# LSH-masked attention in front of two feed-forward blocks: the hash projection of a head in four matmuls, its sum and comparison on other engines, and a new order of the attention

## The chip, the cores and the metric

The kernel runs on one core of a Trainium2 chip. The metric is the device time of one execution in microseconds (us). Five engines work side by side, each through its own queue in order: TensorE (PE) does matmuls and transposes, VectorE (DVE), ScalarE (ACT) and GpSimd (POOL) do elementwise work, SyncE (SP) issues nearly all DMAs.

## The reference

Attention over 2 x 8 heads with 768 rows of 64, where a query sees only the keys that fall in its hash bucket (six signs of a random projection), then two feed-forward blocks of 512 to 2048 to 512 over 1536 tokens:

```python
q_bits = (np.einsum('bhsd,dk->bhsk', q, proj) > 0).astype(np.int64)
k_bits = (np.einsum('bhsd,dk->bhsk', k, proj) > 0).astype(np.int64)
powers = 2 ** np.arange(n_bits)
q_bucket = np.sum(q_bits * powers, axis=-1)
k_bucket = np.sum(k_bits * powers, axis=-1)
mask = q_bucket[:, :, :, None] == k_bucket[:, :, None, :]
scores = scale * np.matmul(q, k.transpose(0, 1, 3, 2))
scores = np.where(mask, scores, -1000000000.0)
attn = softmax(scores); out = np.matmul(attn, v)
h = x @ w_in;  y = (h * np.tanh(softplus(h))) @ w_out      # first block (mish)
h = y @ w_in2; z = (elu(h)) @ w_out2                       # second block
```

## The kernel before, in words

All matmul operands are held as a rounded high part and a low part, the rest (types F32R), and a product is made of hi x hi, hi x lo and lo x hi.

*Attention.* The 16 heads are worked through in tiles of 128 query rows, 6 per head, 96 in all. `prepare(g)` readies head g: q and k come in together (rw), are split into z (high and low), and four DMAs spread z into the operand qkt. `project` (L433) multiplies z by the table sp in six matmuls of 384 columns into one PSUM bank pj: three products times two halves of the rows. One DVE instruction (`bits`, L447) compares the bank with 0 and turns the result into two rows of marks per bit, and four small DMAs (mk) carry these into qkt. They make the masked pairs of the score matmul so negative that the later maximum cuts them to one constant. Head 0 goes another way, without those DMAs.

Per tile: `scores`, four matmuls (st, L511); on DVE the maximum (L514) and its negative (nb, L517); on ACT the exponential (L519). Per pair of tiles: three groups of four transposes (tu, L570); of each group ACT casts the high part (pth, L575) and DVE subtracts the low part (ptl, helper line L260), and four value matmuls (xt, L583) use them. xt is copied out by ACT (xr), moved by DMA, summed and divided by POOL, and split into x_hi and x_lo. tu and st have two PSUM buffers each; xt and pj share two.

*Feed-forward.* Weights arrive as packed doubles (wraw) and are unpacked by `convert`, per unit in five instructions on DVE and two each on ACT and POOL (L299 to L325). Units 0, 1 and 2 are converted while the attention still runs. Then `moe` runs the two blocks (h, L696), 2220 matmuls of 512 columns.

*Order.* Every instruction is an `Op` of a planner (`Plan.run`) that knows a cost per engine, its inputs and its buffers. At each step it takes, for each engine, the ready op of the lowest priority number, and emits the program in that order. The priority of an attention op is the tile's number plus `OFF[name]` plus `ODD[name][tile % 6]` (function `order`, and `at` inside `prepare`). These tables thus set the order on every engine.

At the start, POOL clears 384 columns of x_lo (L657), ten warm-up matmuls (warm, L665) read them, and then the first head follows.

Of the kernel before, what the change touches and what calls it, by code (L numbers as in the profile page):

```python
# [9 lines left out]
F32 = mybir.dt.float32  # L10
# [191 lines left out]
def kernel(ctx, tc, qk, v, w, tab, out):  # L202
# [13 lines left out]
    NB = 6  # L216
# [136 lines left out]
    def attention(p, ap, dp, pss, pst, psx, h_r):  # L353
        ident = ap.tile([128, 128], F32, name="ident")
        cst = ap.tile([128, 3 + NR], F32, name="cst")
        sp = ap.tile([128, 2, 192], F32R, name="sp")
        least, value, small = cst[:, 0:1], cst[:, 1:2], cst[:, 2 + NR:3 + NR]
# [19 lines left out]
        bits_r = ring(2, [128, HS], F32R, "bits")  # L377
# [24 lines left out]
        def prepare(g):  # L402
# [33 lines left out]
            o = pj_op = p.op({PE: 1050}, project, [lo, first[0]], [z, pj], at('pj'))  # L436
# [212 lines left out]
        def setup():  # L649
            nc.vector.memset(f32(sp), 0.0)  # L650
# [415 lines left out]
```

## Time and profile before

| what | us |
|---|---|
| median of 3 timed runs | 744.91 (744.44 to 745.0) |
| the profiled execution, its own time | 746.06 |
| its span from first to last instruction | 744.3 |
| PE busy in the span | 733.9 |
| DVE, ACT, POOL busy | 596.4, 446.7, 389.9 |

The profile is of one execution. Busy time counts an instruction from its start to its end; neighbouring matmuls overlap, so their cost is read from start to start. The attention takes about the first 239 us, the feed-forward blocks the rest. The granted TensorE clock is full in all slices of the profile.

### The profile page before, as it was taken

The page shows a single profiled execution, that of the slowest core. Times are in us where ns is not written, and L with a number is a line of the kernel's source. Part 1 is how long each engine was busy: PE and PEld are TensorE (multiplying, and loading weights), DVE is VectorE, ACT ScalarE, POOL GpSimd, SP SyncE. Part 2 cuts the span into 40 slices and gives each one's busy share as a digit, 9 for nine tenths or more (in the row PEclk, how much of TensorE's full clock was granted, in tenths as well). Part 3 has the DMA queues.
Part 4 walks back from the last instruction along what each step waited for, and adds up shares of the span by engine and source line. Part 5 has one row for each costly group of instructions (what it writes and reads, how often), then busy time and mean ns, then how long its engine had stood idle before and what let it go on. Part 6 is the DMA issues. An engine that isn't in the chain of part 4 may idle for free.

```text
span 744.3 us, 11114 instructions
## 1 busy us (share of the span) xinstructions
PE 733.9 (99%) x3900; PEld 638.3 (86%) x3900; DVE 596.4 (80%) x1103; ACT 446.7 (60%) x871; POOL 389.9 (52%) x323
## 2 busy tenths in 40 slices
PE   8998999999999999999999999999999999999998
PEld 7998999999998878888888888888888888888887
DVE  7899999899997987487677868987665977979872
ACT  5787888888886665543353336568555554635530
POOL 4336726635657664636346274988425355263620
PEclk9999999999999999999999999999999999999999
DMA  7785866767620122122111212311201111113113
GB/s 199 195 208 151 209 148 171 189 162 193 174 63 1 58 86 85 37 83 79 57 57 56 86 59 83 107 64 58 85 28 58 57 57 57 56 62 108 58 59 112
DMA packets 26984, 72.90 MB, mean 98 GB/s; under 512 B 6048, under 2 KB 7216, under 8 KB 26928
## 3 DMA queue, kind: packets, MB, share of 16 engines
q1 hardware_dynamic: 26784, 72.17, 33.7%
q8 instruction: 31, 0.51, 0.3%
q14 instruction: 25, 0.20, 0.1%
q10 hardware_dynamic: 144, 0.01, 0.0%
HBM read 45.76 MB, written 3.19 MB: 66 GB/s over the span
## 4 chain that ended last, share of the span: by engine, by line
PE 88%; DVE 7%; ACT 3%; issue 1%; DMA 0%; POOL 0%; SPq 0%; DVEq 0%; ACTq 0%; POOLq 0%
PE h L696 47%; PE h_b L696 15%; PE xt L583 8%; PE st L511 7%; PE tu L570 7%; PE pj L433 2%; DVE ptl L260 2%; DVE pt L514 1%; ACT pt L519 1%; DVE g L260 1%; DVE T L260 1%; PE warm L665 0%; DMA rr<-dr 0%; ACT pth L575 0%; DVE x_lo L260 0%
## 5 line engine op out<-in xcount | busy, mean ns | idle before, releaser
L696 PE MATMUL h<-g,w 128*128 128x512 f32 x1140 | 264.9, 389 | 1.3 <-DVE g L260 1.3
L696 PEld LDWEIGHTS h<-g,w 128*128 128x128 f32 x1140 | 213.7, 188 | 46.4 <-DVE g L260 2.1
L696 PE MATMUL h<-x_hi,w 128*128 128x512 f32 x384 | 124.0, 390 | 0.0
L260 DVE TENSOR_TENSOR ptl<-tu,pth 128x512 fp32r<-128x512 f32 x144 | 96.1, 686 | 13.0 <-ACT pth L575 11.9
L260 POOL TENSOR_TENSOR wt<-wt,w 128x512 f32<-128x512 f32 x40 | 51.9, 1298 | 92.6 <-DVE c L309 52.7
L575 ACT CAST pth<-tu 128x512 fp32r<-128x512 f32 x144 | 79.9, 587 | 28.3 <-PE tu L570 27.7
L519 ACT ACTIVATE pt<-pt,nb 128x768 f32<-128x768 f32 x96 | 90.5, 944 | 8.3 <-DVE nb L517 7.9
L317 POOL TENSOR_TENSOR wt<-wt,ws 128x512 f32<-128x512 f32 x24 | 31.0, 1295 | 116.1 <-DVE ws L312 116.1
L514 DVE TENSOR_SCALAR_CACHE_REDUCE pt<-st 128x768 f32<-128x768 f32 x96 | 89.1, 950 | 1.4 <-PE st L511 0.9
L696 PEld LDWEIGHTS h<-x_hi,w 128*128 128x128 f32 x384 | 72.1, 188 | 15.0 <-DVE pt L514 0.2
L511 PE MATMUL st<-qkt 76*128 76x384 f32 (+1 forms) x384 | 81.5, 344 | 1.2 <-DVE pt L514 0.7
L570 PE MATMUL tu<-ident,pt 128*128 128x128 f32 x576 | 80.0, 274 | 2.5 <-DVE ptl L260 2.4
L583 PE MATMUL xt<-pth,vt 128*128 128x256 f32 x288 | 79.2, 304 | 0.0
L973 DVE TENSOR_TENSOR y_acc<-h,y_acc 128x512 f32<-128x512 f32 x71 | 48.1, 687 | 34.8 <-PE h L696 34.7
L696 PE MATMUL h<-x_lo,w 128*128 128x512 f32 x192 | 74.7, 389 | 0.0
L255 ACT CAST w<-wt 128x512 fp32r<-128x512 f32 x64 | 39.7, 625 | 56.6 <-DVE wt L307 29.3
L583 PE MATMUL xt<-ptl,vt 128*128 128x256 f32 x288 | 73.1, 282 | 0.4 <-DVE ptl L260 0.4
L570 PEld LDWEIGHTS tu<-ident,pt 128*128 128x128 f32 x576 | 66.7, 141 | 7.7 <-issue 2.6
L511 PEld LDWEIGHTS st<-qkt 76*128 76x128 f32 (+1 forms) x384 | 64.1, 189 | 2.4 <-DVE pt L514 1.5
L325 POOL TENSOR_TENSOR w<-wt,ws 128x512 fp32r<-128x512 f32 x40 | 52.5, 1314 | 6.1 <-DVE ws L312 3.9
L304 DVE SCALAR_TENSOR_TENSOR wt<-wraw,c 128x512 int32<-128x512 int32 x61 | 41.5, 682 | 17.7 <-POOL w L260 13.5
L583 PEld LDWEIGHTS xt<-ptl,vt 128*128 128x128 f32 x288 | 54.7, 190 | 0.8 <-DVE ptl L260 0.6
(112 smaller groups left out, 1325.6 us busy)
## 6 DMA issues: line engine op xcount, KB each, us to landing
wraw<-in_w_dram SPq DMA_DIRECT2D x64, 512.0 KB
qkt<-z SPq DMA_DIRECT2D x30, 384.0 KB
rw<-in_qk_dram SPq DMA_DIRECT2D x16, 384.0 KB
qkt<-z SPq DMA_DIRECT2D x31, 192.0 KB
vr<-in_v_dram SPq DMA_DIRECT2D x8, 384.0 KB
out_dram<-y_acc SPq DMA_DIRECT2D x11, 256.0 KB
rr<-dr SPq DMA_DIRECT2D x14, 192.0 KB
xs<-xr SPq DMA_DIRECT2D x14, 192.0 KB
```

Of the source, the lines that this page charges most:

```text
L255: nc.scalar.copy(out=out, in_=in_)
L260: eng(e).tensor_tensor(out=out, in0=a, in1=b, op=ALU.subtract)
L304: o3 = p.op({DVE: dve(n)}, lambda e: nc.vector.scalar_tensor_tensor(out=ti(), in0=high(), scalar=-0x40000000, in1=bits(b), op0=ALU.bitwise ...
L325: o9 = p.op({POOL: cost}, lambda e: nc.gpsimd.tensor_tensor(out=lo(), in0=t.tile, in1=s.tile, op=ALU.add), [o6, o8], [t, s, w_], prio)
L511: nc.tensor.matmul(st.tile[:, c, 0:HS], lhsT=wt.tile[0:n, q, t * 128:(t + 1) * 128], rhs=wt.tile[0:n, 2 + q, c * HS:(c + 1) * HS], start=( ...
L514: o = max_op = p.op({DVE: dve(S)}, lambda e: nc.vector.tensor_scalar(out=half(pt.tile), in0=st.tile[:, :, 0:HS], scalar1=-MASKED / SCALE, ...
L519: o = p.op({ACT: act(S, False) + 196}, lambda e: nc.scalar.activation(out=pt.tile, in_=pt.tile, func=AF.Exp, bias=nb.tile, scale=SCALE, ac ...
L570: nc.tensor.transpose(tu.tile[:, k, j], pt.tile[:, (2 * b + k) * 128:(2 * b + k + 1) * 128], ident)
L575: o = p.op({ACT: act(512)}, lambda e, tu=tu, ks=ks: nc.scalar.copy(out=hi.tile[:, ks], in_=flat(tu)), [o], [tu, hi], order(i, 'hi'))
L583: nc.tensor.matmul(xt.tile[:, 0:TH], lhsT=vt.tile[:, k, g % 2], rhs=m.tile[:, k], start=(k == 0 and j == 0), stop=(k == NKT - 1 and j == 1))
L696: nc.tensor.matmul(t.tile, lhsT=w_.tile[:, a, k], rhs=r, start=(start and n == 0), stop=(stop and n == 3 * len(ks) - 1), skip_group_check= ...
L973: y = p.op({DVE: dve(n)}, lambda e, ya=ya, t=t: nc.vector.tensor_tensor(out=ya, in0=t.tile, in1=ya, op=ALU.add), [x, Y[m, c]], [t], prio)
```

## The change

For heads 1 to 15 `project` uses a second table sq. It has the high part of the hash table in 24 columns at 32 and the low part at 96 (first plane), and the high part alone (second plane). A matmul of z's high part with 128 columns of the first plane gives hi x hi in rows 0 to 63 and hi x lo in rows 64 to 127 of the bank; a matmul of z's low part with the second plane adds lo x hi to rows 0 to 63. So two products of two halves are four matmuls in place of six. What is left to do, the sum of the two halves of the bank, is: ACT copies rows 64 to 127 to SBUF (`both`), DVE adds rows 0 to 63 to it, and POOL does the comparison that was DVE's. The marks lie in 64 rows in place of 128, in 24 adjacent rows per half. sq is cleared and filled by POOL at the start. OFF and ODD have new numbers, and a new table EDGE adds one for single ops of the first and last tiles and heads. Head 0 is as it was.

```diff
+EDGE = {'rr5': -16.0, 'rr11': -4.0, ...
-OFF = {'rr': 66.5, 'rh': 5.75, 'cp': 25.0, ...
+OFF = {'rr': 752.0, 'rh': 151.25, 'cp': -64.75, ...
...
+        sq = ap.tile([128, 2, 160], F32R, name="sq")
...
+        def spread_table(e):
+
+            for a, j, at in ((0, 0, 32), (1, 0, 32), (0, 1, 96)):
+                nc.gpsimd.tensor_copy(out=sq[:, a, at:at + 4 * NB].rearrange("p (s n) -> p s n", s=2),
+                                      in_=f32(sp[:, j, 64:128]).rearrange("p (s n) -> p s n", s=2)[:, :, 0:2 * NB])
...
-        bits_r = ring(2, [128, HS], F32R, "bits")
+        bits_r = ring(2, [64, HS], F32R, "bits")
+        both_r = ring(1, [64, HS], F32, "both")
...
-            return i + OFF[name] + ODD.get(name, (0,) * NQ)[i % NQ]
+            return i + OFF[name] + ODD.get(name, (0,) * NQ)[i % NQ] + EDGE.get(f"{name}{i}", 0)
...
             def project(e):
                 n = 0
+                if g:
+                    for a in range(2):
+                        for c in range(2):
+                            nc.tensor.matmul(pj.tile[:, 0:HS], lhsT=sq[:, a, 32 * (1 - c):32 * (1 - c) + 128],
+                                             rhs=z.tile[:, a, c * HS:(c + 1) * HS], start=(n == 0), stop=(n == 3))
+                            n += 1
+                    return
...
-            o = pj_op = p.op({PE: 1050}, project, [lo, first[0]], [z, pj], at('pj'))
+            o = pj_op = p.op({PE: 700 if g else 1050}, project, [lo, first[1 if g else 0]], [z, pj], at('pj'))
...
-                o = p.op({DVE: dve(HS)}, lambda e: nc.vector.tensor_scalar(
-                    out=bits.tile, in0=pj.tile[:, 0:HS], scalar1=least, scalar2=value, op0=ALU.is_ge, op1=ALU.mult),
-                    [o], [pj, bits], at('bits'))
+                both = Buf(both_r, f"both{g}")
+                h = p.op({ACT: act(HS)}, lambda e: copy(e, both.tile, pj.tile[64:128, 0:HS]), [o], [pj, both], at('pc'))
+                o = p.op({DVE: dve(HS)}, lambda e: nc.vector.tensor_tensor(
+                    out=both.tile, in0=pj.tile[0:64, 0:HS], in1=both.tile, op=ALU.add), [h], [pj, both], at('bits'))
+                o = p.op({POOL: 150 + 1.07 * HS}, lambda e: nc.gpsimd.tensor_scalar(
+                    out=bits.tile, in0=both.tile, scalar1=cst[0:64, NV:NV + 1], scalar2=cst[0:64, NV + 1:NV + 2], op0=ALU.is_ge, op1=ALU.mult),
+                    [o], [both, bits], at('bits'))
...
             nc.vector.memset(f32(sp), 0.0)
+            nc.gpsimd.memset(f32(sq), 0.0)
...
+            first.append(p.op({POOL: 400}, spread_table, [first[0]], (), -1e3))
```

Three places of the order on the engines. The first is DVE in a middle head, around the old comparison and the new addition of head 8 (names carry the number of the head or tile, then a buffer number). Before:

```order
L260 TENSOR_TENSOR ptl39_1624<-tu39_0_1595,pth39_1606 128x512
L260 TENSOR_TENSOR ptl39_1624<-tu39_1_1600,pth39_1606 128x512
L447 TENSOR_SCALAR bits8_1646<-pj8_1630,cst_83 128x384
L260 TENSOR_TENSOR ptl39_1624<-tu39_2_1640,pth39_1606 128x512
L260 TENSOR_TENSOR ptl41_1677<-tu41_0_1648,pth41_1666 128x512
```

and of the change:

```order
L261 TENSOR_TENSOR ptl39_1630<-tu39_1_1606,pth39_1617 128x512
L535 TENSOR_SCALAR pt43_1649,mx43_1648<-st43_1634 128x768
L466 TENSOR_TENSOR both8_1651<-pj8_1624,both8_1651 64x384
L261 TENSOR_TENSOR ptl39_1630<-tu39_2_1642,pth39_1617 128x512
L261 TENSOR_TENSOR ptl41_1681<-tu41_0_1653,pth41_1667 128x512
```

The maximum of tile 43 now stands in front of the head's DVE step, whose two inputs are the bank and ACT's copy.

The second is PE in head 7, between two transpose groups of tile pair 42, 43 that share a PSUM buffer (tu43_0 and tu43_2). Before:

```order
L570 MATMUL tu43_0_1725<-ident_82,pt43_1593 128x128 x2
L570 MATMUL tu43_1_1730<-ident_82,pt42_1583 128x128 x2
L570 MATMUL tu43_1_1730<-ident_82,pt43_1593 128x128 x2
L511 MATMUL st44_1741<-qkt7_1320 128x384 x4
L583 MATMUL xt41_1751<-pth41_1666,vt6_1353 128x256
L583 MATMUL xt41_1751<-ptl41_1677,vt6_1353 128x256
```

six more such xt rows follow there before tu43_2; of the change:

```order
L591 MATMUL tu43_1_1749<-ident_82,pt43_1649 128x128 x2
L532 MATMUL st47_1758<-qkt7_1326 128x384 x4
L604 MATMUL xt41_1733<-pth41_1667,vt6_1375 128x256
L604 MATMUL xt41_1733<-ptl41_1681,vt6_1375 128x256
L604 MATMUL xt41_1733<-pth41_1667,vt6_1375 128x256
L604 MATMUL xt41_1733<-ptl41_1681,vt6_1375 128x256
L591 MATMUL tu43_2_1779<-ident_82,pt42_1603 128x128 x2
```

Four value matmuls stand between the groups in place of eight.

The third is DVE where the first weight unit is converted (wt0 from wraw0). Before:

```order
L299 TENSOR_SCALAR wt0_988<-wraw0_581 128x512
L304 SCALAR_TENSOR_TENSOR wt0_988<-wraw0_581,wt0_988 128x512
L447 TENSOR_SCALAR bits5_999<-pj5_975,cst_83 128x384
L260 TENSOR_TENSOR ptl21_973<-tu21_1_961,pth21_954 128x512
L260 TENSOR_TENSOR ptl21_973<-tu21_2_993,pth21_954 128x512
```

and of the change:

```order
L466 TENSOR_TENSOR both5_956<-pj5_941,both5_956 64x384
L538 TENSOR_SCALAR nb25_990<-mx25_969 128x1
L549 RECIPROCAL rc3_992<-sm3_793 128x6
L261 TENSOR_TENSOR ptl21_1003<-tu21_0_958,pth21_988 128x512
L261 TENSOR_TENSOR ptl21_1003<-tu21_1_974,pth21_988 128x512
L305 SCALAR_TENSOR_TENSOR wt0_801<-wraw0_545,wt0_801 128x512
L535 TENSOR_SCALAR pt27_1031,mx27_1030<-st27_996 128x768
L261 TENSOR_TENSOR ptl21_1003<-tu21_2_1016,pth21_988 128x512
```

The two conversion instructions stood together; the first now comes some 26 DVE rows earlier, and the second behind the second ptl of tile pair 20, 21.

## Rows read from the trace of the kernel before

**Rows 1.** The page: busy time by engine, and the chain that ended last.

```profile
PE 733.9 (99%) x3900; PEld 638.3 (86%) x3900; DVE 596.4 (80%) x1103; ACT 446.7 (60%) x871; POOL 389.9 (52%) x323
...
PE 88%; DVE 7%; ACT 3%; issue 1%; DMA 0%; POOL 0%; SPq 0%; DVEq 0%; ACTq 0%; POOLq 0%
```

**Rows 2.** Table by stage: stretch, its length, then busy time (instructions) per engine, clock.

```profile
60.54:74.06 13.52, 11.45 (x88) 11.03 (x87) 13.48 (x27) 9.69 (x23) 7.68 (x6) 1.00 0.47 126
...
128.14:141.66 13.52, 13.52 (x105) 13.39 (x104) 12.19 (x30) 11.43 (x26) 7.28 (x5) 1.00 0.76 188
...
195.74:209.00 13.26, 13.26 (x101) 12.81 (x100) 13.09 (x31) 11.58 (x26) 5.96 (x5) 1.00 0.59 150
209.00:224.00 15.00, 14.66 (x103) 13.29 (x103) 14.49 (x42) 12.70 (x29) 10.89 (x10) 1.00 0.26 75
```

**Rows 3.** Timeline, 117 to 123 us, PE and ACT: start, duration, what.

```profile
118.42 1.21 PE L433 MATMUL pj<-z,sp 128*128 128x384 f32 x6
119.47 1.03 PE L570 MATMUL tu<-ident,pt 128*128 128x128 f32 x8
...
122.00 1.06 PE L570 MATMUL tu<-ident,pt 128*128 128x128 f32 x8
...
122.64 1.08 ACT L575 CAST pth<-tu 128x512 fp32r<-128x512 f32 x2 [1.12 <-PE tu L570]
```

**Rows 4.** Chain of waits in order of time: start, time on the chain, what.

```profile
86.00 1.43 PE xt L583 x12
...
110.01 1.42 PE st L511 x8
...
222.83 0.87 PE tu L570 x8
```

**Rows 5.** Timeline of the first 18 us; in brackets idle time before, and who ended it.

```profile
1.25 0.42 POOL L657 MEMSET x_lo<- 128x384 f32 x1
...
1.72 3.57 PE L665 MATMUL warm<-x_lo 128*128 128x384 f32 x10 [1.72 <-POOL x_lo L657]
...
16.44 1.05 ACT L575 CAST pth<-tu 128x512 fp32r<-128x512 f32 x2
...
17.79 0.66 PE L570 MATMUL tu<-ident,pt 128*128 128x128 f32 x4 [0.34 <-DVE ptl L260]
```

**Rows 6.** Groups by line and shape: count, busy us, mean ns, idle before.

```profile
L255 ACT COPY xr<-xt 128x256 f32<-128x256 f32 x42 | 15.8, 377 | 1.9 <-PE xt L583 1.9
...
L636 DVE TENSOR_TENSOR xr<-xt,xr 64x256 f32<-64x256 f32 x6 | 2.6, 427 | 0.2
...
L447 DVE TENSOR_SCALAR bits<-pj,cst 128x384 fp32r<-128x384 f32 x15 | 10.1, 674 | 2.7 <-PE pj L433 2.6
...
L533 POOL COPY rb<-rc 128x128 f32<-128x128 f32 x6 | 2.3, 396 | 5.6 <-DVE rc L528 5.2 <-DVE nb L517 0.4
...
L257 POOL CAST z<-rw 128x768 fp32r<-128x768 f32 x14 | 12.0, 858 | 64.6 <-DMA qkt<-z 44.8 <-PE tu L570 11.8 <-DMA xs<-xr 4.9
...
L519 ACT ACTIVATE pt<-pt,nb 128x768 f32<-128x768 f32 x96 | 90.5, 944 | 8.3 <-DVE nb L517 7.9
```

**Rows 7.** The stall at 65 us: timeline of DVE, POOL, PE; then L304's later group.

```profile
63.50 2.22 DVE L304 SCALAR_TENSOR_TENSOR wt<-wraw,wt 128x512 int32<-128x512 int32 x1
...
63.14 2.02 POOL L260 TENSOR_TENSOR vt<-vr,vt 128x768 fp32r<-128x768 f32 x1
...
67.05 0.63 PE L570 MATMUL tu<-ident,pt 128*128 128x128 f32 x4 [2.07 <-DVE ptl L260]
...
L304 DVE SCALAR_TENSOR_TENSOR wt<-wraw,c 128x512 int32<-128x512 int32 x61 | 41.5, 682 | 17.7 <-POOL w L260 13.5 <-POOL w L325 2.5
```

**Rows 8.** PE's waits in the whole span: us in total, times, longest.

```profile
PE h L696 <- DVE g L260: 1.3, 2, 1.1
PE st L511 <- DVE pt L514: 0.7, 2, 0.5
...
PE xt L583 <- DVE ptl L260: 0.4, 1, 0.4
```

More of the change, by code (lines that the diff above doesn't have):

```diff
@@ L52 @@
 GATE = [13, 68, 26]
 WAIT = {'PE': 150, 'ACT': 0, 'DVE': 50, 'POOL': 50, 'SP': 100}
-OFF = {'rr': 66.5, 'rh': 5.75, 'cp': 25.0, 'ld': 10.0, 'sp': 4.75, 'pj': -3.5, 'bits': -19.25, 'mk': -2.0, 'v': -92.25, 'S': -0.25, 'max': 5.25, 'exp': 44.0, 'sum': 56.75, 'eps': 30.25, 'T': -0.5, 'hi': 5.25, 'lo': 4.0, 'R': 7.5, 'pv': 7.25, 'xc': -64.25, 'xa': 17.75, 'xn': 10.0, 'xh': 63.75, 'xm': 40.0}
-ODD = {'lo': [-11.0, 5.0, 4.5, -7.0, 3.0, -0.5], 'T': [0.0, 2.5, -5.0, -2.5, 10.0, -1.5], 'pv': [0.5, -0.5, -3.0, -5.5, -0.5, -2.5], 'exp': [9.0, -0.5, -6.0, 10.0, 4.5, -9.0], 'hi': [0.5, -3.0, -7.5, 6.0, 7.0, -0.5], 'S': [-2.0, -2.5, 1.5, 0.0, -1.0, -2.0], 'xc': [-11.0, 5.5, 6.0, 2.5, -4.5, -0.5], 'max': [7.5, 10.5, -2.5, -7.0, -17.0, 14.0]}
+OFF = {'rr': 752.0, 'rh': 151.25, 'cp': -64.75, 'ld': 521.25, 'sp': -11.0, 'pj': 10.0, 'bits': -582.5, 'pc': -170.0, 'mk': 296.5, 'v': -52.5, 'S': 28.5, 'max': -557.75, 'exp': 626.25, 'sum': -98.75, 'eps': 778.25, 'T': -506.75, 'hi': -79.25, 'lo': -746.5, 'R': -524.75, 'pv': -18.0, 'xc': -373.0, 'xa': -9.25, 'xn': -241.75, 'xh': -203.75, 'xm': 269.0}
@@ L56 @@
+ODD = {'lo': [0.0, -39.5, 1.5, -7.25, -25.75, -15.75], 'T': [-21.0, 9.75, 24.0, 8.25, 10.25, 6.75], 'pv': [-18.0, -365.5, 24.0, -177.0, -8.75, 40.5], 'exp': [0.0, -229.0, -33.5, -3.75, -2.25, 9.5], 'hi': [50.75, -249.5, 26.25, -0.25, -22.0, 0.0], 'S': [-391.0, -12.75, -10.0, -12.75, -11.5, -12.25], 'xc': [7.5, -10.75, -14.0, 0.0, 3.0, -22.5], 'max': [-3.75, 1.0, -41.0, -90.0, -12.25, -28.0]}
 PE, ACT, DVE, POOL, SP = "PE", "ACT", "DVE", "POOL", "SP"
@@ L354, in attention @@
         ident = ap.tile([128, 128], F32, name="ident")
-        cst = ap.tile([128, 3 + NR], F32, name="cst")
+        NV = 3 + NR
+        cst = ap.tile([128, 5 + NR], F32, name="cst")
         sp = ap.tile([128, 2, 192], F32R, name="sp")
+        sq = ap.tile([128, 2, 160], F32R, name="sq")
         least, value, small = cst[:, 0:1], cst[:, 1:2], cst[:, 2 + NR:3 + NR]
@@ L406, in at @@
             def at(name):
-                return pr + OFF[name] if g else -50
+                return pr + OFF[name] + EDGE.get(f"{name}#{g}", 0) if g else -50
             wt, rw, z = Buf(w_r, f"qkt{g}"), Buf(rw_r, f"rw{g}"), Buf(z_r, f"z{g}")
@@ L1034 @@
     vv = v.reshape(B * H // 2, 2, S // 128, 128, D).transpose(0, 3, 2, 1, 4).reshape(B * H // 2, 128, S // 128, 2 * D)
-    tab = np.zeros((2 * D, 3 + 4 * NB), np.float32)
+    tab = np.zeros((2 * D, 5 + 4 * NB), np.float32)
     tab[:, 2 + 4 * NB] = 1e-9
@@ L1042 @@
         tab[c + 32:c + 32 + 2 * NB, 1] = -BIG
+    for c in (0, 32):
+        tab[c:c + NB, 3 + 4 * NB] = tab[c + 3 * NB:c + 4 * NB, 3 + 4 * NB] = TINY
+        tab[c:c + 2 * NB, 4 + 4 * NB] = 1.0
+        tab[c + 2 * NB:c + 4 * NB, 4 + 4 * NB] = -BIG
     units = []
```

3 lines of the change are left out of this document (2 added, 1 removed).

## The prediction

> **What bounds the kernel now.** I read the page first [rows 1]: TensorE (PE) is busy 99% of the span and makes up 88% of the chain that ended last. A busy PE need not be an unbroken one, so the table by stage comes next [rows 2]. In the middle heads the PE column equals the stretch, 13.52 of 13.52 us; VectorE (DVE) has 12.19, ScalarE (ACT) 11.43, GpSimd (POOL) 7.28. The heads on either side of that one read alike, so there one matmul less is one matmul's time less. It is otherwise in three places. At 60.54 PE has 11.45 of 13.52 while DVE has 13.48. In the last heads (195.74 to 224) PE and DVE are both nearly full, 13.26 with 13.09 and 14.66 with 14.49. And in the first 18 us PE waits for others.
>
> What a matmul costs is read from starts, since the durations overlap: a projection starts at 118.42 and the transposes behind it at 119.47 [rows 3], so six matmuls of 384 columns take 1.05 us, 0.175 each. The chain of waits gives the same for the scores (eight in 1.42), 0.12 for a value matmul (twelve in 1.43) and 0.109 for a transpose (eight in 0.87) [rows 4].
>
> **The change, part by part.** Durations are from the one profiled execution, whose span is 744.3 us and whose own time is 746.06; the median of the three timed runs is 744.91, so I make the sum as differences against the span and take them from the median.
>
> *Two matmuls fewer per head.* 15 of 16 heads go from six to four matmuls: 2 x 0.175 = 0.35 us each, 5.25 us in all. This counts only where PE is the one that is waited for. The projections of heads 1 and 2 lie before 18 us, where PE stands for DVE (idle before 17.79 [rows 5]); that of head 15 lies where DVE is as full as PE [rows 2]. I count 12 heads: **-4.2 us**; with all 15 it would be -5.25.
>
> *The sum and the comparison.* The old comparison (bits, one DVE instruction of 0.67 us per head) becomes an ACT copy of 64 x 384, a DVE addition of 64 x 384 and a POOL comparison [rows 6]. No row has these shapes. The copy lies between 0.377 (256 columns) and about 0.53 (512 columns, two casts in 1.05 [rows 5]); I take 0.48, as it is 384 columns. The addition lies between 0.427 (64 x 256, the same kind with one input in PSUM) and the 0.674 of bits; I take 0.55. The comparison lies between 0.396 and 0.858, the nearest POOL rows with one input; I take 0.55. In a head shortened to 13.17 us ACT would have 11.43 + 0.48 = 11.9, DVE 12.2 less 0.1, POOL at most 7.28 + 0.86 = 8.1: all below PE, so I cost them at nothing, and PE's own work is the cover. The way from projection to scores grows by the copy and the comparison, 0.9 to 1.4 us with their hand-overs. Against that the new order puts 10.3 us of PE work between the end of a projection and the next head's first scores in the middle heads, where it was 8.7 (counted in the two orders with the prices above): 1.6 us more, so the masks should not be late. Four mask DMAs per head stay four; they now wait for POOL, and what stands behind them on SP's queue (the next load, the reciprocal's two DMAs) moves with them. The load is for a head two further on, and the reciprocals serve a pair of heads that is already done, so neither is near PE.
>
> *The start.* POOL now clears the new table (320 columns) ahead of what the warm-up matmuls wait for. The memset of 384 columns takes 0.42 [rows 5], so this one takes 0.35, and the warm-up, the first projection and the first scores move by as much. Behind the first maximum DVE now has an addition that waits for ACT in front of the second maximum; I put 0.1 on it, between 0 and 0.55. **+0.45 us.**
>
> *The stall at 65 us.* PE stands 2.07 us before 67.05. Its releaser is a ptl subtraction of DVE; what was late stands ahead of that: one instruction of the first weight unit's conversion (L304), 2.22 us from 63.50, where the 61 later ones have 0.682. It ends 0.56 us behind POOL's subtraction of 63.14 to 65.16 [rows 7]. In the old order it stands ahead of the second ptl subtraction of its pair of tiles, in the new one behind the second, ahead of a maximum and the third. The transposes that wait for the third have some 1.4 us of PE work to spare, by my count. So a wait for one short POOL instruction (a cast has 0.858 [rows 6]) is covered, and one for a long one nearly. **-2.1 us.** If the cover is gone it stays at 2.1.
>
> *The rest of the order.* The last twelve score tiles are issued in another sequence, and the second and third weight units are converted later. PE's waits there are about 1.9 us together: 1.3 on DVE's g, 0.4 of xt on ptl and 0.2 of st (its other 0.5 is in the first 18 us) [rows 8]. The DVE work up to the first gate activations is the same, and DVE is what that stretch is made of, so I take **0**, between -1.9 (all gone) and +1.5 (as much again as one g wait).
>
> Sum: -4.2 + 0.45 - 2.1 + 0 = -5.85 us; 744.91 - 5.85 = **739.1 us**.
>
> **The rivals.**
>
> *B. The stall stays, or moves.* When DVE wants a two-input instruction on SBUF data while POOL works, it waits: L304 ended only after POOL's subtraction had [rows 7]. The new order has one POOL instruction more per head, and DVE also takes over the first x_hi cast, again next to POOL's longest instructions. For it: the conversion still meets POOL's z instructions. Against: the 1.4 us of cover. Price 2.1: 741.2 us. The Trainium skill's "SBUF — State Buffer", section "SBUF: two separate sides", says that the pair of ports that VectorE and GpSimd share is an exclusive lock held for the whole instruction, and that the loser fully blocks. The 2.22 against 0.68 agrees with it.
>
> *C. The order is tighter than the chain.* From a transpose group to the reuse of its PSUM buffer two groups later the chain is: transposes end to cast, 122.64 - 122.00 - 0.44 = 0.20 [rows 3]; cast to the release of PE, 17.79 - 16.44 = 1.35 [rows 5]; 1.55 in all. The old order gives it 2.09 us in the middle heads (four transposes, four scores, eight value matmuls), the new one 1.61 (four value matmuls). If ACT or DVE is busy when its turn comes, PE waits, each head. At 0.35 per head the matmuls' gain is gone and only the start and the stall are left: 744.91 - 1.65 = 743.3. For: 0.06 us of slack. Against: single places of the old order have 1.61 too, without a wait in the trace.
>
> *D. A wait on DVE takes the place of the matmuls: slower.* DVE's addition waits for ACT's copy, which stands behind an exponential (0.94 [rows 6]) and can stand behind a cast (0.53); everything behind the addition on DVE, the ptl subtractions above all, waits along, and PE's transposes wait for those. DVE has 13.52 - 12.19 = 1.33 us idle per head. Up to that nothing is lost against before; with 1.47 (exponential and cast in front of each copy) the head becomes 12.19 + 1.47 = 13.66, 0.14 more than now, 1.8 us over 13 heads: 744.91 + 1.8 + 0.45 = 747.2. It decides from 1.33 us of wait per head. For: in-order queues, DVE at 12.1 of 13.17. Against: a maximum that waits for PE stands in front of the addition, so ACT has had its time.
>
> *E. The end gains too.* All 1.9 us of waits behind 195 us go: 737.2. For: the order there is new tile by tile. Against: DVE is full there.
>
> That the change doesn't do what it says is excluded: the new order has 30 matmuls fewer.
>
> **How the numbers follow.** A (forecast) 0.50, B 0.16, C 0.12, D 0.10, E 0.12. I forecast A: 739.1. The range goes down to E with the start's 0.45 and head 15's 0.35 gained too, 737.2 - 0.8 = 736.4, say 736.3, and up to C, 743.4; outside stay D and the tails, under 2 in 10. No change is within 0.2%, 1.5 us, about what a measurement can tell. Faster takes A, B, E and half of C: 0.84. Same is most of the other half and the near part of D, 0.06. Slower is D's far part with the unforeseen, 0.10.
>
> **What would show it.** Right: the pj group with 66 matmuls (6 + 60); middle heads of about 13.17 us with PE equal to the stretch; the first L305 no longer followed by idle PE; warm-up start near 2.07. Wrong: repeated PE waits on ptl in the middle heads (C); DVE waiting for ACT's both over 1 us a head (D); PE idle next to a POOL instruction and a long DVE one (B). A forecast of this kind fails as a whole if middle heads stay at 13.5 us.

## The result and the profile after

| | us |
|---|---|
| before, median of 4 runs beside it | 744.67 (743.84 to 745.0) |
| the changed kernel, median of 4 runs | 749.65 (749.12 to 752.31) |
| ratio, 95% interval | 1.0076, 1.005 to 1.0101 |
| its profiled execution: own time, span | 749.91, 748.1 |

Slower by 0.8%, where 739.1 (736.3 to 743.4) was forecast. The page of the changed kernel, the lines that answer to [rows 1]:

```profile
PE 732.0 (98%) x3870; PEld 635.6 (85%) x3870; DVE 597.8 (80%) x1103; ACT 454.0 (61%) x886; POOL 416.1 (56%) x342
...
PE 77%; DVE 6%; DMA 5%; POOL 4%; issue 3%; ACT 3%; SPq 1%; POOLq 0%; DVEq 0%; ACTq 0%
```

There are 30 matmuls fewer, and PE has 77% of the chain that ended last instead of 88%: POOL and DMAs, which had 0%, now have 9% of it. The table by stage, with the columns of [rows 2]:

```profile
60.54:74.06 13.52, 12.57 (x92) 11.83 (x91) 13.31 (x30) 10.37 (x24) 8.32 (x6) 1.00 0.59 148
113.57:126.74 13.17, 9.37 (x60) 9.10 (x59) 7.58 (x17) 7.00 (x17) 9.20 (x6) 0.87 0.62 154
126.74:139.91 13.17, 13.17 (x101) 13.08 (x100) 12.21 (x30) 11.88 (x26) 4.22 (x4) 1.00 0.62 158
```

The third row is what was forecast: a middle head in 13.17 us, with PE equal to the stretch. The second row, one head earlier, is not: PE works 9.37 of 13.17 us, and the granted clock of the stretch is 0.87, so part of it ran at the lower of the two levels (1.2 instead of 2.4 GHz).

Where the time went can be put in one table. From the start of a PE instruction at about a given time I take off what all PE work ahead of it costs at the prices from start to start; what is left is PE's lost time so far. The price of each kind of matmul is the median of the kernel before (0.32 us for a warm-up matmul). (e13 is the last version of the experiments.)

| lost by, us | 20 | 70 | 110 | 130 | 180 | 200 | end |
|---|---|---|---|---|---|---|---|
| before | 5.12 | 8.14 | 8.26 | 8.35 | 8.59 | 8.91 | 14.03 |
| changed | 6.85 | 9.99 | 10.50 | 16.21 | 16.68 | 18.18 | 23.09 |
| e13 | 6.40 | 7.68 | 8.85 | 9.08 | 9.83 | 10.62 | 15.33 |

The changed kernel loses 9.06 us more than before and saves 30 x 0.175 = 5.25 of work: +3.8, the difference of the spans (748.1 and 744.3). Of the 9.06, 1.73 are lost by 20 us, 5.62 between 110 and 130, 1.18 between 180 and 200. The place at 116 us in the timeline, by engine (start, duration, what, in brackets the idle time before and who ended it):

```profile
107.90 0.59 SPq L639 DMA_DIRECT2D xr<-xr  x1
...
114.28 1.83 POOL L641 TENSOR_TENSOR xr<-xr,xs 128x768 f32<-128x768 f32 x1 [1.36 <-DMA xr<-xr]
116.19 2.19 POOL L645 TENSOR_TENSOR xr<-xr,rr 128x768 f32<-128x768 f32 x1
118.31 0.82 POOL L258 CAST vt<-vr 128x768 fp32r<-128x768 f32 x1
...
118.40 1.15 DVE L258 CAST x_hi<-xr 128x768 fp32r<-128x768 f32 x1 [3.75 <-POOL xr L645]
119.47 0.14 DVE L538 TENSOR_SCALAR nb<-mx 128x1 f32<-128x1 f32 x1
119.53 0.68 DVE L261 TENSOR_TENSOR ptl<-tu,pth 128x512 fp32r<-128x512 f32 x1
...
120.27 0.97 PE L591 MATMUL tu<-ident,pt 128*128 128x128 f32 x4 [3.80 <-DVE ptl L261]
...
121.25 0.41 PE L604 MATMUL xt<-ptl,vt 128*128 128x256 f32 x1
121.46 0.41 PE L604 MATMUL xt<-pth,vt 128*128 128x256 f32 x1
```

Read it upwards. PE stands 3.80 us for a ptl of DVE. DVE's queue stood 3.75 us at a cast that PE doesn't need: x_hi of the third pair of heads, which the new plan gave to DVE and which needs POOL's product L645. POOL was late because its sum waited for a transfer that SP had issued 6.4 us earlier, at 107.90; in the kernel before SP issued the same transfer at 104.64, and POOL's sum did not wait. Behind the stop the value matmuls start 0.21 us apart instead of 0.12.

The new operations in the groups (count, busy us, mean ns, idle before):

```profile
L468 POOL TENSOR_SCALAR bits<-both,cst 64x384 fp32r<-64x384 f32 x15 | 24.8, 1651 | 44.1 <-DVE both L466 31.8 <-DMA qkt<-z 8.2 <-DVE nb L538 4.1
...
L466 DVE TENSOR_TENSOR both<-pj,both 64x384 f32<-64x384 f32 x15 | 8.2, 544 | 0.3 <-ACT both L256 0.2
L256 ACT COPY both<-pj 64x384 f32<-64x384 f32 x15 | 7.1, 476 | 4.2 <-PE pj L444 3.9
L258 DVE CAST x_hi<-xr 128x768 fp32r<-128x768 f32 x2 | 2.3, 1148 | 4.1 <-POOL xr L645 4.1
```

Copy and addition cost what was taken (0.48, 0.55). POOL's comparison costs 1.651 us, three times the 0.55. In some heads it also stands in a queue. In head 13 of the changed kernel, its engines' rows (the projection's four matmuls start from 175.72 to 176.26):

```profile
177.56 0.48 ACT L256 COPY both<-pj 64x384 f32<-64x384 f32 x1
...
178.22 0.55 DVE L466 TENSOR_TENSOR both<-pj,both 64x384 f32<-64x384 f32 x1
...
178.01 1.86 POOL L261 TENSOR_TENSOR x_lo<-xr,x_hi 128x768 fp32r<-128x768 f32 x1
179.82 1.86 POOL L261 TENSOR_TENSOR vt<-vr,vt 128x768 fp32r<-128x768 f32 x1
181.65 1.66 POOL L468 TENSOR_SCALAR bits<-both,cst 64x384 fp32r<-64x384 f32 x1
```

The sum is there at 178.8, the comparison ends at 183.3: 7.05 us from the start of the last projection matmul. Before, the same way took 1.05 us in nearly every middle head; in the changed kernel it takes 4.2 to 5.0 us in the heads 8 to 12 and over 6 in the heads 2, 7, 13 and 15, where the comparison starts 1.7 to 2.9 us behind its input, because POOL has a pair's or a new v's work first. PE's waits, the lines that answer to [rows 8]:

```profile
PE tu L591 <- DVE ptl L261: 4.9, 3, 3.8
...
PE h L719 <- DVE g L261: 2.0, 1, 2.0
PE st L532 <- DVE pt L535: 1.4, 3, 0.6
PE st L532 <- DMA qkt<-bits: 1.3, 3, 0.6
PE xt L604 <- DVE ptl L261: 0.5, 1, 0.5
```

The line on qkt<-bits is new: scores that wait for their masks, in the heads 3, 13 and 14.

### The profile page after: what moved, and what is told of

Same layout as the page of the kernel before. It is cut to its first block, busy times and chain, and to the rows that moved or that the text cites. A ratio compares the mean times of both kernels' runs of the same rounds, so it can differ in the third digit from the quotient of the medians.

```text
span 748.1 us, 11110 instructions
## 1 busy us (share of the span) xinstructions
PE 732.0 (98%) x3870; PEld 635.6 (85%) x3870; DVE 597.8 (80%) x1103; ACT 454.0 (61%) x886; POOL 416.1 (56%) x342
## 4 chain that ended last, share of the span: by engine, by line
PE 77%; DVE 6%; DMA 5%; POOL 4%; issue 3%; ACT 3%; SPq 1%; POOLq 0%; DVEq 0%; ACTq 0%
PE h L719 47%; PE h_b L719 15%; PE xt L604 5%; PE tu L591 5%; PE st L532 4%; DMA qkt<-bits 1%; DMA rw<-in_qk_dram 1%; DVE ptl L261 1%; ACT pth L596 1%; DVE x_lo L261 1%; ACT pt L540 1%; DMA xr<-xr 1%; PE pj L444 1%; POOL z L261 1%; POOL xr L641 1%
## 5 line engine op out<-in xcount | busy, mean ns | idle before, releaser
L261 DVE TENSOR_TENSOR ptl<-tu,pth 128x512 fp32r<-128x512 f32 x144 | 94.2, 683 | 9.7 <-ACT pth L596 8.0
L532 PE MATMUL st<-qkt 76*128 76x384 f32 (+1 forms) x384 | 83.5, 345 | 3.1 <-DVE pt L535 1.4
L604 PE MATMUL xt<-pth,vt 128*128 128x256 f32 x288 | 80.9, 308 | 0.2 <-POOL vt L261 0.2
L305 DVE SCALAR_TENSOR_TENSOR wt<-wraw,c 128x512 int32<-128x512 int32 x61 | 41.5, 682 | 17.8 <-POOL w L261 13.3
L604 PEld LDWEIGHTS xt<-pth,vt 128*128 128x128 f32 x288 | 54.7, 190 | 0.5 <-POOL vt L261 0.5
```

Of the source, the lines that this page charges most:

```text
L261: eng(e).tensor_tensor(out=out, in0=a, in1=b, op=ALU.subtract)
L305: o3 = p.op({DVE: dve(n)}, lambda e: nc.vector.scalar_tensor_tensor(out=ti(), in0=high(), scalar=-0x40000000, in1=bits(b), op0=ALU.bitwise ...
L532: nc.tensor.matmul(st.tile[:, c, 0:HS], lhsT=wt.tile[0:n, q, t * 128:(t + 1) * 128], rhs=wt.tile[0:n, 2 + q, c * HS:(c + 1) * HS], start=( ...
L604: nc.tensor.matmul(xt.tile[:, 0:TH], lhsT=vt.tile[:, k, g % 2], rhs=m.tile[:, k], start=(k == 0 and j == 0), stop=(k == NKT - 1 and j == 1))
```

## The experiments

Each kernel was timed against the kernel before on the same chip; medians of before were 744.36 to 744.79. "The changed kernel" is the one of 749.65. Differences between two kernels are differences of medians; taken through the ratios to the kernel before they come out up to 1.6 us otherwise where the two were timed on different occasions. The expectations count a stop of PE from start to start, which gives 0.15 to 0.25 us more than the idle time in the views.

**First four.** e1 puts the one cast on POOL:

```diff
-lambda e: copy(e, x_hi[:, kt, to], xe.tile)
+lambda e: copy(POOL if (b, kt) == (0, 2) else e, x_hi[:, kt, to], xe.tile)
```

> The changed kernel with one instruction on another engine: the high half of the third pair of heads (x_hi <- xr, 128x768, which stood in DVE's queue at 118.40 us) is cast by POOL at the same place of the program; every other instruction and its order stay. Theory (the 9 us that the changed kernel loses against its saved matmuls are mostly this one place): DVE no longer stands 3.75 us behind POOL's product and 1.15 us in the cast, PE's idle 3.80 us at 120.27 goes, and so do the 1.6 us that the matmuls took longer behind it at a granted clock of 0.87; 5.6 us in all, so 749.65 - 5.6 = 744.1 (743.3 to 745), clock 1.0 in that stretch. Rival 1 (the late thing is the transfer xr <- xr and whatever waits for it; the cast is only where it shows): PE waits somewhere else in the same head, over 748. Rival 2 (the clock falls there whatever PE waits for): 745.7 and the clock still near 0.87.

Measured: 748.07 (ratio 1.0041, 1.0026 to 1.0055). The stop is gone and the clock of its profile is 1.000, yet only 1.6 of the 5.6 us came back (2.6 by the ratios). PE's waits in e1, first line of the view:

```profile
PE st L532 <- DMA qkt<-bits: 4.4, 6, 1.3
```

and POOL's timeline in the head behind the old stop:

```profile
120.03 1.84 POOL L261 TENSOR_TENSOR x_lo<-xr,x_hi 128x768 fp32r<-128x768 f32 x1
121.82 1.86 POOL L261 TENSOR_TENSOR vt<-vr,vt 128x768 fp32r<-128x768 f32 x1
123.65 1.65 POOL L468 TENSOR_SCALAR bits<-both,cst 64x384 fp32r<-64x384 f32 x1
```

So rival 1 is right in its number, barely, but its mechanism is another: PE waits for masks (1.3 us in three places in the changed kernel, 4.4 in six here). The stop had given POOL and SP the time to catch up. POOL's queue is not the whole of it. In the heads 9 and 13 of e1 the comparison starts 3.4 and 2.9 us behind its input, but in head 12 it starts at once, and SP issues the masks late, behind z and other transfers:

```profile
161.31 1.65 POOL L468 TENSOR_SCALAR bits<-both,cst 64x384 fp32r<-64x384 f32 x1 [6.57 <-DVE both L466]
...
165.47 2.37 SPq L474 DMA_DIRECT2D qkt<-bits  x3
...
168.44 0.73 SPq L474 DMA_DIRECT2D qkt<-bits  x1
```

e2 moves the comparison:

```diff
-lambda e: nc.gpsimd.tensor_scalar(out=bits.tile, in0=both.tile, ...
+lambda e: nc.vector.tensor_scalar(out=bits.tile, in0=both.tile, ...
```

> The changed kernel with the comparison of the 15 later heads (bits <- both, 64x384) on DVE instead of POOL, at the same place of the program. Theory: the comparison takes 0.43 to 0.67 us there instead of 1.65, the mask DMAs leave about 1.1 us earlier, and the scores' waits for them (0.65 at 43 us, 0.30 at 56, 0.77 at 188, 0.36 at 198, 2.1 together) go; the event at 116 to 124 us stays: 747.6. Rival (DVE, 12.21 us of a middle head's 13.17, is what another 0.5 us per head hurts): PE waits for ptl appear, a middle head lasts over 13.3 us, and the time is 750 to 755.

Measured: 750.64 (1.0068, 1.004 to 1.0096), the rival's number, though not clear of the changed kernel's. No score waits for masks any more, but DVE's comparison takes 718 ns on average (467 in the median, up to 1958), and PE waits for DVE's ptl in eight places (3.3 us together) and for its maxima (2.9). The event at 116 us did not stay as expected: DVE was so late that it stood only 0.27 us at the cast, and PE worked 12.36 of the 13 us from 113 at a full clock. In this order DVE has no room for the comparison.

e3 clears sq behind the columns of x_lo.

> The changed kernel with the 320 columns of sq cleared behind the columns of x_lo that the warm-up multiplies, not ahead of them. Theory (the warm-up waits for POOL's clearing, and the start as a whole comes 0.3 later for it): warm-up from 1.72 instead of 2.02, and 0.3 us less in all: 749.3. Rival (the 1.7 us lost up to 20 us come from the order of the first head, which waits for DVE and the DMAs and not for the warm-up): warm-up 0.3 earlier, time 749.65 as it was.

Measured: 749.68 (1.0063, 1.0043 to 1.0082); the warm-up begins at 1.72, and the time is as it was: the rival's number. But 0.3 us is less than these runs can tell, so this does not show that the memset costs nothing.

e4 is the new projection in the old order:

```diff
-EDGE, OFF, ODD of the changed kernel (tables left out here)
+EDGE = {}; OFF, ODD of the kernel before, with 'pc': -19.25
-CH = {... 'xh': ('POOL', 'DVE')}
+CH = {... 'xh': ('POOL',)}
```

> The projection in four matmuls with the planner's numbers of the kernel before (no EDGE table; the copy of the low half gets the number of the comparison), and x_hi on POOL alone as the kernel before had it in all seven pairs. Theory (the matmul saving is real, 15 x 2 x 0.175 = 5.25 us, and what ate it is the new order): 744.67 - 5.25 + 0.3 at the start + up to 2.1 of mask waits = 739.7 to 741.8. Rival (the new operations themselves, the comparison of 1.65 us on POOL above all, hurt wherever they stand): 744 to 750, with waits for the mask DMAs in most heads.

Measured: 769.0 (1.0317, 1.0287 to 1.0347), beyond both. The first lines of PE's waits:

```profile
PE tu L591 <- DVE ptl L261: 5.3, 9, 1.1
PE tu L591 <- DVE nb L538: 3.1, 6, 0.6
PE pj L444 <- POOL z L261: 3.0, 3, 1.3
```

With the three-step sum this order is 24 us slower than the kernel before; the new order brings most of that back. Without it the change would have been a loss of 3%.

**The masks.** e5 takes their wait away:

```diff
-in_=f32(bits.tile[r])
+in_=zm[0:2 * NB]
```

> The kernel of e1 (third pair's x_hi on POOL), and the 60 mask transfers read a table of zeros written once at the start instead of bits, so that they wait for no comparison; copy, addition and comparison still run. What it leaves out: the masks, so every key counts. Theory (what is left of e1's loss is scores waiting for their mask transfers: 1.46 us at 43, 0.91 at 129, 0.66 and 1.10 at 169, 0.79 at 186, 0.55 at 196, 5.5 together, because the way from the last projection matmul to the end of the comparison went from 1.05 us to between 3.2 and 7.6): 748.07 - 5.5 = 742.6 (741.8 to 743.6), no score waits for a transfer of bits. Rival (PE is faster by 0.35 us per head and any next wait takes over at once, as ptl on DVE): over 745.5, with new waits on DVE in the same heads.

Measured: 744.04 (0.9993, 0.9984 to 1.0002), 4.0 under e1: nearer to the theory than to the rival, but 1.4 short of it and outside both ranges. New waits took some of it back, 0.67 us before 67.10 and 0.71 before 85.15, both for DVE.

e6 asks what makes the comparison dear:

```diff
-scalar1=cst[0:64, NV:NV + 1], scalar2=cst[0:64, NV + 1:NV + 2]
+scalar1=0.0, scalar2=1.0
```

> The kernel of e1, and POOL's comparison takes its two scalars as numbers (0.0 and 1.0) instead of a value per partition. What it changes: the two kinds of bits are no longer told apart, so the masks are others. It measures the price of the operation by itself. Theory (the per-partition scalars make it dear): 0.4 to 0.6 us instead of 1.65; the comparisons end 1.1 us earlier, and of the six waits for masks 0.36 us is left: 743 (742.2 to 744.5). Rival 1 (the price is that of the comparison itself): 1.65 as before, 748.1. Rival 2 (cheap, but the queue of POOL ahead of it makes the masks late): 0.4 to 0.6 us and yet waits of over 3 us for the masks, 745.5 to 747.

Measured, the comparison's group in e6 (count, busy us, mean ns, idle before):

```profile
L468 POOL TENSOR_SCALAR bits<-both 64x384 fp32r<-64x384 f32 x15 | 22.5, 1500 | 36.4 <-DVE both L466 32.2 <-DVE nb L538 4.2
```

1.50 us: the price is that of the operation, rival 1; the scalars per partition are 0.15 of it. The time was 746.41 (1.002, 1.0005 to 1.0035), 1.7 under e1, where rival 1 had none. PE still waits 3.4 us for masks in e6, so what gave the 1.7 is not shown.

e7 leaves the price and changes the queue: x_hi and x_lo of a pair (up to head 12) are kept back until the next comparison has been emitted, and x_hi of all pairs is on POOL. The edit in part:

```diff
+            if o.tag == "x":
+                kept.append(o)
+                continue
             o.fn(o.eng)
+            if o.tag == "bits" or kept and o.tag == "wraw":
+                for x in kept:
+                    x.fn(x.eng)
+                kept = []
```

> The changed kernel with both DVE casts of x_hi on POOL, and in POOL's order the two operations of each pair (x_hi, 0.82 us, and x_lo, 1.84 us), which nothing needs before the next phase, put behind the comparison that follows them. Theory (in the heads in which a pair ends the comparison stands behind these 2.66 us: at 123.65 us in e1 although its input was there at 120.21): there it starts 2.6 us earlier, the waits at 129 and 186 go, those of the heads between, in which SP issues the masks late (43, 169, 196), stay: 748.07 - 1.7 = 746.4 (745.5 to 747.3). Rival (z and its split, behind the comparison in the same queue, set the end): projections wait for z, and 748 to 749.

Measured: 744.55 (0.9996, 0.998 to 1.0011), 3.5 under e1, twice the 1.7 expected and below both ranges. The head that was shown for e1, in the timeline of e7:

```profile
120.04 0.55 DVE L476 TENSOR_TENSOR both<-pj,both 64x384 f32<-64x384 f32 x1
120.69 1.65 POOL L478 TENSOR_SCALAR bits<-both,cst 64x384 fp32r<-64x384 f32 x1 [0.67 <-DVE both L476]
122.30 0.82 POOL L268 CAST x_hi<-xr 128x768 fp32r<-128x768 f32 x1
```

The comparison now follows its input. Scores wait for masks once, 0.8 us, instead of six times, 4.4 us (it is the one at 43 us; those at 169 and 196, which I had put down to SP, went too: SP comes to the masks of head 12 0.8 us behind the comparison's end here, 2.5 in e1). The way from the last projection matmul to the end of the comparison is still 4.25 us in e7's heads 8 to 10, 3.2 more than before, and PE does not wait there.

**The cast by itself.** e8 moves it in the kernel before, e16 puts it back into e7:

```diff
-lambda e: copy(e, x_hi[:, kt, to], xe.tile)
+lambda e: copy(DVE if (b, kt) == (0, 2) else e, x_hi[:, kt, to], xe.tile)
```

> The kernel before, with the same cast (x_hi of the third pair) moved from POOL to DVE at the place where the plan has it, and nothing else. Theory (a cast on DVE behind a product of POOL stops DVE's queue): DVE comes to it at 114.30 us, the product ends at 115.87, the cast takes 1.15 as in the changed kernel, so that DVE's later work comes 2.7 us later, and of this 0.9 us is DVE's slack in the head: 744.4 + 1.8 = 746.2 (745.3 to 747.1). Rival (DVE's slack and the buffers take it up): 744.2 to 744.8.

> The kernel of e7, with the third pair's cast x_hi back in DVE's queue where the changed kernel has it (x_lo stays behind the comparison). It prices that one place alone, in a kernel whose masks are no longer late: e1, which took it away with the masks late, gave only 1.6 us. Theory (the place costs DVE's wait of 3 to 4 us behind POOL's product, less DVE's slack, and the slower matmuls behind PE's stop): 744.55 + 4 = 748.5 (747 to 750), PE idle of over 2 us near 116 us. Rival (what the changed kernel lost there is the same microseconds that the masks would have cost, and alone the place is small): 744.5 to 746.

Measured: e8 746.85 (1.0042, 1.0017 to 1.0067), e16 749.7 (1.0054, 1.0033 to 1.0076), the theory both times. In e8 DVE and PE read, in their timeline,

```profile
114.20 1.15 DVE L257 CAST x_hi<-xr 128x768 fp32r<-128x768 f32 x1 [1.25 <-POOL xr L624]
...
117.13 1.97 PE L570 MATMUL tu<-ident,pt 128*128 128x128 f32 x8 [1.80 <-ACT pt L519]
```

and the table by stage has

```profile
113.50:127.00 13.50, 11.70 (x75) 11.39 (x74) 10.41 (x23) 9.19 (x20) 7.68 (x6) 0.87 0.44 103
```

In e16 the table by stage has

```profile
113.00:126.00 13.00, 10.47 (x69) 10.20 (x69) 8.67 (x21) 7.49 (x17) 8.13 (x6) 0.87 0.58 153
```

and the timeline

```profile
116.24 1.15 DVE L268 CAST x_hi<-xr 128x768 fp32r<-128x768 f32 x1 [2.49 <-POOL xr L656]
```

and in PE's waits the first line is

```profile
PE tu L602 <- DVE ptl L271: 4.3, 3, 2.5
```

One cast in DVE's queue costs 5.1 us in e7 (4.3 by the ratios) and 2.5 in the kernel before (3.1), where DVE waited 1.25 us for the product in place of 2.49. Four kernels now form a square (e7 and e16 also have the first pair's cast on POOL):

| us | comparison behind the pair's work | ahead of it |
|---|---|---|
| third pair's cast on DVE | 749.65 (changed) | 749.7 (e16) |
| on POOL | 748.07 (e1) | 744.55 (e7) |

By the medians either fault alone costs 3.5 to 5.1 us, and both together no more than the dearer one. The ratios (1.0076, 1.0054, 1.0041, 0.9996) put both together at 6.0 us, the faults alone at 4.3 and 3.4: less than the sum again, but by no more than their intervals allow. That one fault hides the other rests on the traces, where the masks' waits went from 1.3 to 4.4 us when the stop was taken away. Mending one of the two does not show what it was worth.

**What the saved matmuls are worth.** e9 gives e7 its six matmuls back:

```diff
-                    for a in range(2):
+                    for a, b in ((0, 0), (0, 1), (1, 0)):
```

> The kernel of e7, and each of the 15 later projections issues six matmuls again instead of four (the extra two multiply by columns that the comparison then reads as part of its sums, so the bits are others; copy, addition, comparison and the order stay). It measures what the 30 saved matmuls are worth where the mask's way is no longer late. Theory (PE is the limit of every stretch between the few waits): 30 x 0.175 = 5.25 us more, less what those two heads with waits absorb: 744.55 + 4.7 = 749.2 (748.3 to 750), middle heads 13.52. Rival (DVE, ACT and the masks set the pace as much as PE does): under 747.5.

Measured: 748.22 (1.0054, 1.0042 to 1.0066), 3.67 more than e7, between theory (4.7) and rival (under 3). A middle head is 13.50 us with PE full, as expected. Between the two profiles it is 4.4 (spans of 747.2 and 742.8): by the account of the table e9 loses 0.8 us less than e7. PE's waits are 8.2 us in e9's view and 10.1 in e7's; that its masks and DVE had more time would explain this, and was not tried by itself.

**Towards a better version.** In e7 PE still waits 1.2 us at 86 us for a ptl behind the first of these two (timeline):

```profile
83.06 2.34 DVE L323 SCALAR_TENSOR_TENSOR ws<-wraw,ws 128x512 f32<-128x512 uint32 x1
...
83.00 1.85 POOL L271 TENSOR_TENSOR z<-rw,z 128x768 fp32r<-128x768 f32 x1
```

DVE's product, 0.68 us elsewhere, began 0.06 us behind POOL's subtraction and ended 0.55 us behind its end: the mechanism of [rows 7]. e10 moves the comparison of head 1 behind v on POOL and the addition of head 3 ahead; e11 moves the product two DVE operations back (for the third weight tile that put it behind its reader, whose low part was then summed from older values, in e11 and e12); e12 does all.

> The kernel of e7, with two moves: the comparison of head 1 and its four mask transfers behind the first pair's low half of v on POOL (where it now stands at 11.87 us, 1.65 us ahead of z and v, with two tiles for both), and the addition of head 3 on DVE three instructions earlier (its copy was there at 33.57 us, the addition started at 35.42). Theory: the 0.46 us that PE waits for vt at 18.5 us and a part of the 0.97 ahead of it at 17 go, and the wait for the masks at 43.0 us (0.98) goes: 744.55 - 1.7 = 742.9 (742.2 to 743.6). Rival (at the start the wait for ptl of DVE is the limit, and POOL's order changes nothing; head 3's masks wait for SP): 744.3 to 744.8.

> The kernel of e7, with the last DVE product of each weight tile that is converted during the attention (ws <- wraw, 128x512, three of them) two operations later in DVE's order, behind two subtractions ptl. Theory (such an instruction on DVE that starts within a POOL instruction on the same memory lasts until that one has ended: 2.34 us at 83.06 against a POOL split that ended at 84.85, 2.06 us at 195.68 against one that ended at 197.19, but 0.68 in the changed kernel at 84.27): ptl comes 2 us earlier, the waits of PE at 84.6 (1.39) and 197.3 (0.96) go, and the product, started at 84.3 between two POOL instructions and at 197, takes about 0.7 us: 744.55 - 2.2 = 742.4 (741.6 to 743.4). Rival (the product's 2 us then stop the reductions of the scores behind it, and PE waits for those): 744 to 745.

> The moves of e7, e10 and e11 together. Theory (the waits are apart in time and add up): 744.55 - 1.7 - 2.2 = 740.7 (739.7 to 742), under the kernel before by over 2 us. Rival (each move frees DVE or POOL for another collision of the same kind): 742.5 to 744.5.

Measured: e10 751.28 (1.0084, 1.0054 to 1.0114), outside both ranges: the scores of head 1 begin at 20.5 us, and with the comparison moved they waited 2.7 us for its masks, at a granted clock of 0.74 between 19 and 27 us. I had taken the wrong time for the masks' due date. e12 747.7 (1.0047, 1.0028 to 1.0066), outside both ranges too, carries the same wait (1.3 and 1.0 us in its trace). e11 743.03 (0.9977, 0.9964 to 0.9989), within the theory's bounds.

> The kernel of e11 with the third weight tile's product left where the plan has it (in e11 it was moved too, and PE's wait at 227.5 us grew from 0.63 to 1.77 behind it); all of the computation is done. Theory (DVE's product, kept out of POOL's splits, gives 1.39 at 84.6 and 0.96 at 197.3 back): 743.03 - 1.1 = 742.0 (741.2 to 743.2), under the kernel before by 0.2 per cent or more. Rival (the tail takes it back: in e7, where that product stood in its old place, PE waited 2.13 us for g at 270, in e11 0.99): 743.0 to 744.

> The kernel of e13 and head 3's addition on DVE three instructions earlier, as in e10. Theory (the wait for head 3's masks at 43 us, 0.98 in e7, is this addition's place in DVE's queue): 0.5 to 1.0 under e13. Rival (that wait comes and goes with the transfers: in e11 it was not there at 43 but 0.46 at 55): the same as e13 within 0.5.

e13 moves the first two products only and does the whole computation: **743.3** (0.9977, 0.9957 to 0.9996), the same ratio as e11's. That is under both kernels, by 1.1 us under before. PE's waits in it, three lines of the view:

```profile
PE h L749 <- DVE g L284: 2.0, 1, 2.0
PE tu L619 <- DVE ptl L284: 1.3, 2, 0.8
...
PE st L560 <- DMA qkt<-bits: 0.5, 2, 0.3
```

That is the rival's range, 0.1 us outside the theory's: PE's wait for g is back at 2.0 us. e14 measured 744.91 (1.0002, 0.9986 to 1.0017): head 3's addition ahead costs 1.6 us, with a new wait of PE for DVE's maximum (1.2 us). Neither expectation had that.

**The old order once more.** e15 is e4 with the comparison on DVE, in the plan too:

> The kernel of e4 (four matmuls, the planner's numbers of the kernel before), and the comparison planned and done on DVE, so that POOL has nothing new but the table at the start. Theory (the comparison of 1.65 us on POOL is what cost e4 most of its 24 us: there PE waits for z from POOL, 1.1 to 1.5 us each at 104, 106, 150 and 152): 748 to 756, no wait of PE for POOL's z over 0.5 us. Rival (the copy, the addition and their waits cost that order as much, wherever the comparison is): 760 to 770.

Measured: 769.67 (1.0328, 1.0299 to 1.0356), the rival. POOL is relieved, and PE waits for DVE instead (us, times, longest):

```profile
PE tu L591 <- DVE ptl L261: 14.1, 15, 2.6
PE st L532 <- DVE pt L535: 3.6, 7, 1.5
```

So the 24 us of e4 do not come from the comparison's engine. I had set the priority of the new copy myself there; another might do better, and that wasn't tried.

## Why the prediction was wrong, point by point

- **Two matmuls fewer per head, -4.2: right.** There are 66 projection matmuls and middle heads of 13.17 us with PE full; e9 puts the 30 matmuls at 3.7 us (4.3 by the ratios) where the masks are in time.
- **The sum and the comparison at nothing: the first step that failed.** Copy and addition were sized to 0.01 us. The comparison was bounded by 0.396 and 0.858, casts and copies on POOL; it takes 1.651, outside both ends. The bound was no bound, because no elementwise row of POOL had an operation with two scalars. With 1.65 the way to the masks would have been forecast to grow by 2.0 to 2.5 us against 1.6 of room, a wait. But that test was not the right one either: the way grew by 3.2 us in the heads 8, 10 and 12 of the changed kernel, and PE waited for masks in none of them, so the order before had slack of its own that I had left out. The price alone did not make the masks late there. What I had not counted is the place: POOL's busy time of one head (7.28; the middle heads before have 5.50 to 9.08) does not say what stands ahead of the comparison in its queue, nor ahead of the masks in SP's. In head 13 the way grew by 6.0. Against e1, e5 prices all waiting for the masks at 4.0 us, and e7, which also takes the first pair's cast off DVE, gets 3.5 back.
- **The casts of x_hi that the plan moved to DVE: the second step that failed.** Rival B names the first of the two, as a collision with POOL worth 2.1 us. What counts is that the cast needs POOL's product, so that DVE's whole queue waits for POOL and for a transfer behind it. The order of the two engines showed this; I costed the instruction and not its input. In the changed kernel's trace this place is 5.62 of the 9.06 us lost; alone it costs 5.1 us (e16, 4.3 by the ratios), and of them a part is the clock, which averaged 0.87 over that head.
- **The stall at 65 us, -2.1: half right in the trace, wrong in the sum.** L305 still takes 1.62 us, and the stop behind it is 0.6 instead of 2.07. But the 2.07 belonged to that execution. In e8, which is the same program up to there, POOL's subtraction came earlier and L304 took no longer than the later ones (timeline of e8):

```profile
63.57 0.69 DVE L304 SCALAR_TENSOR_TENSOR wt<-wraw,wt 128x512 int32<-128x512 int32 x1
...
65.60 0.63 PE L570 MATMUL tu<-ident,pt 128*128 128x128 f32 x4 [0.49 <-DVE ptl L260]
```

  The profiled execution stood 1.15 us over the median, so the term took from the median a stall that the median executions need not have. What it should have been is not known: about -0.9 if the 1.15 us are this stall, nothing if most executions are like e8's. Nothing was gained in any case: from 20 to 70 us the changed kernel loses 3.14, the profiled execution before 3.02 and e8, by the same account, 1.42, for new waits stand there (0.48 us for masks at 44, 0.33 behind the first cast at 62, 0.62 behind L305 at 68).
- **The start, +0.45: too small.** In the changed kernel's trace 1.73 us more are lost by 20 us, in e1, e7 and e16 1.1 to 1.4. The warm-up starts 0.30 later (2.02; 0.35 was forecast), and PE waits 0.80 us for ptl and 0.82 for maxima of DVE where the kernel before has 0.34 and 0.47. The wait for ptl stays at 0.80 when POOL's comparison is moved behind v (e10) and when the memset is moved (e3); what makes DVE late there stays open.
- **The rest, 0: right in the sum.** Behind 200 us the two kernels lose 5.12 and 4.91 us, though the waits are others (for g 1.3 before, 2.0 now). The 1.18 us between 180 and 200 hold the masks' waits at 189 and 199 (0.61 and 0.20).
- **The rivals.** D (slower, 747.2) had the sign and not the mechanism: DVE waited 0.2 us in all for ACT's copies. C did not come: no repeated wait for ptl in the middle heads. B's collisions are real (e7, e11) and worth one or two us. The rival that was missing is POOL as a bound through its order while it is busy 56%.
- **What is left.** With both faults out e7 stands at 744.55, still 5.5 us over the forecast: about 2.1 are the stall's term, 0.9 the start beyond its 0.45, 1.2 the wait at 86 us, of which e13 takes 0.7 away. The rest are smaller waits that were not taken one by one.

The Trainium skill's "GPSIMD Engine Reference", section "4.1 Engine selection", says that elementwise work with one input runs at about line rate on GpSimd. The cast of 768 columns agrees (0.82 us, 1.07 ns per column), the comparison doesn't (4.3 ns per column, 3.9 with plain numbers in e6). The Trainium skill's "SBUF — State Buffer", section "SBUF: two separate sides", says that of a GpSimd instruction and a VectorE one that needs the ports they share, the one that starts first holds them for its whole instruction and the other blocks. The traces agree: the cast x_hi on DVE lasts 1.15 us in the changed kernel's two and in e8, and each time it begins 0.09 us behind POOL's cast of v (118.31 to 119.13 in the changed kernel) and ends 0.42 us behind that one's end.

## What to carry to other kernels

When work moves to another in-order engine, price its place and not only its duration: list what stands ahead of it in that queue, what those instructions wait for, and who needs the result when. A new kind of operation has no bound from rows of other kinds; leave it open upwards. Take gains at single stalls only if they are in more than one execution, and expect one fault to hide another: a stop gives the engines behind it time to catch up.

## What the runs showed that I had not expected

- A POOL comparison with a product, 64 x 384, takes 1.65 us, a cast of twice the columns 0.82.
- Two late things need not add up: 749.65 with both, 749.7 and 748.07 with one, 744.55 with none (the medians; by the ratios this is not clear of noise).
- The clock: stops of PE of 3.80, 2.53 and 1.80 us near 116 us (changed, e16, e8) all stand in stretches with a granted clock of 0.87, while the 2.07 us at 65 us before [rows 7] left it at 1.00 [rows 2]. Nor does one program always pay alike: e8's eight executions have a mean granted clock of 0.999 or 1.0 in six and 0.997 and 0.993 in two, the profiled one among these. The length of a stop alone does not tell what it costs.
- One program's executions differ by where DVE's and POOL's instructions meet: L304 took 2.22 us in one trace and 0.69 in another with the same order up to there.
